# Moving the start addresses of the buffers that TensorE reads

## The chip, the cores and the metric

The kernel runs on one core of one Trainium2 chip. The metric is the device time of one execution in microseconds, the median of several. A profiled execution gives, beside its own time, a trace: start and duration of the instructions of every engine. In the trace PE is TensorE at its matmuls, PEld is TensorE loading the stationary operand of a matmul (LDWEIGHTS, which overlaps the matmul ahead of it), DVE is VectorE, ACT is ScalarE, POOL is GpSimd, and SP issues the DMAs.

## The reference

A gated mix of an attention block and a GEGLU feed-forward block, both over the same input `x` of 2048 rows by 448 columns, in float32:

```python
g = _sigmoid((x * gate_w).sum(-1, keepdims=True))
a = _A_ref(x, A_wqkv, A_wo)        # 16 heads of 28: softmax(q k^T * 28**-0.5) v, then @ wo
b = _B_ref(x, B_w_gate, B_w_up, B_w_down)   # (gelu(x @ w_gate) * (x @ w_up)) @ w_down, 1792 wide
return g * a + (1 - g) * b
```

## The kernel before

**Precision.** Most products are made of two-part operands: each float32 value is split into a rounded part and the remainder, both of type float32r, and `PAIRS` names the 11 products of parts that make one full product over the 448 rows. So a block of 128 x 512 results is 11 matmuls one after the other into one PSUM tile. Only the product of exponentials and V is plain float32; its matmuls stand in the trace as two records each.

**Stages.** First, `X` (both parts of x transposed, resident for the whole kernel) is loaded and Q and K are computed (`pqk`, 28 blocks) and written to DRAM in two parts; then V and the gate's sums (`pv`). Second comes attention: per head, `Q` and `K` (114 rows: four copies of the 28 values and two rows for a bound) are loaded into one of two sets of buffers, head by head in turn. For every 128 keys and half of the 2048 queries there are two matmuls `sc` (K block stationary, Q moving) into a PSUM tile of 1024 columns, of which there are three; ScalarE makes exponentials `pt` of it (12 buffers). After every eighth such tile come 32 records of `po` (V stationary, `pt` moving) for the 512 keys of the section before. `fill` strews the up-projection `pu` (weights `half` stationary, `X` moving) between the scores, two matmuls at a time, so that a section of eight score tiles holds 16 `sc` and 11 `pu` matmuls. Third comes the feed-forward part: `pg` (gate projection, again `half` stationary and `X` moving), its gelu multiplied by the stored `u`, the split product `hl2`, and `pd`: `hl2` stationary, the split down weights `w` moving, six matmuls for two weight tiles. In between, `project` multiplies the attention output `ohl` (stationary) with `WO` (moving), also into a `pd` tile.

**Weights in turn.** `load_half` (up and gate weights) and `load_f` (down weights) each go round three buffers, which are called `half0` to `half2` and `w0` to `w2`.

**The order.** The matmuls keep the order in which they are written (`keep_in_program_order`); the other engines' work is placed by the framework's dependencies and the pools' buffers.

**Where the buffers lie.** Each tile is a stretch of bytes in every SBUF partition. The allocator stacks the tiles of a pool, so a tile's first byte follows from the sizes of the tiles ahead of it. The widths in the code before carry `LINE = 16` extra floats (64 bytes) for several tiles, by which the start addresses are spread. Start addresses modulo 512 bytes, of the tiles which TensorE reads, worked out from the program's allocation:

| tile | role in its matmul | before | after |
|---|---|---|---|
| X | moving in pqk, pu, pg; stationary in pv | 352 | 352 |
| WQK | stationary in pqk | 352 | 352 |
| WV | moving in pv, rows of 1800 bytes | 352 | 352 |
| Q (two buffers) | moving in sc | 32, 32 | 352, 352 |
| K (two buffers) | stationary in sc | 32, 96 | 352, 352 |
| half (three buffers) | stationary in pu, pg | 352, 416, 480 | 352, 352, 352 |
| V | stationary in po, 128 bytes further per head | 32 | 352 |
| pt | moving in po | 352 | 352 |
| hl2 (four buffers) | stationary in pd | 32 | 352 |
| w first part (three buffers) | moving in pd | 288, 352, 416 | 352, 352, 352 |
| w second part | moving in pd | 32, 96, 160 | 352, 352, 96 |
| ohl | stationary in pd of `project` | 288 | 352 |
| WO, its eight blocks | moving in pd of `project` | 288 and 32 in turn | 352 |

Within X, Q, K, half and hl2 every matmul reads from an offset that is a multiple of 512 bytes, so the residue of the tile is that of each of its matmuls' operands. "Residue" below means this start address modulo 512.

Of the kernel before, what the change touches and what calls it, by code (L numbers as in the profile page):

```python
# [7 lines left out]
F32 = mybir.dt.float32  # L8
F32R = mybir.dt.float32r
I32 = mybir.dt.int32  # L10
AF = mybir.ActivationFunctionType
OP = mybir.AluOpType
# [4 lines left out]
S, D, H, DH, F = 2048, 448, 16, 28, 1792  # L17
P = 128
TB = 512
# [9 lines left out]
NB = 3  # L29
ORDER = (2, 3, 1, 4, 0, 5, 6)  # L30
NR = 4 * DH + 2
LINE = 16
VW = 450
SCALE = DH ** -0.5
BOUND = 20.0
# [8 lines left out]
def gated_mix(ctx: ExitStack, tc: tile.TileContext, xT, wqk, wvg, wg, wu, wd, wo, sel, ident, out):  # L44
    nc = tc.nc

    def mm(o, lhsT, rhs, start, stop):
        tc.keep_in_program_order(nc.tensor.matmul(o, lhsT, rhs, start=start, stop=stop))  # L48
# [13 lines left out]
    fw = ctx.enter_context(tc.tile_pool(name="fw", bufs=2))  # L62
# [1 line left out]
    vp = attn.enter_context(tc.tile_pool(name="vp", bufs=1))  # L64
    V = vp.tile([P, NKT, H, 32], F32, name="V")
    kq = attn.enter_context(tc.tile_pool(name="kq", bufs=1))
    heads = [tuple(kq.tile([NR, S + n * LINE], F32R, name=f"{x}{i}")[:, 0:S] for x, n in (("Q", i), ("K", 4 * i)))
             for i in range(2)]
    for _, K in heads:
        nc.gpsimd.memset(K[96:].bitcast(F32), 1.0)  # L70
    nc.gpsimd.memset(V[:, :, :, DH:], 1.0)
# [124 lines left out]
    with tc.If(bounded < 1):  # L196
        with ExitStack() as ph:
            gp = ph.enter_context(tc.tile_pool(name="gp", bufs=2))
# [4 lines left out]
            for h in range(H):  # L203
                Q = gp.tile([4 * DH, S], F32R, name="gQ")
                K = gp.tile([4 * DH, S], F32R, name="gK")
# [3 lines left out]
                for i in range(NT):  # L209
                    p = gps.tile([P, S], F32, name="gsc")  # L210
# [14 lines left out]
    gp = ctx.enter_context(tc.tile_pool(name="gp", bufs=1, side="right"))  # L225

    halves = {}

    def load_half(src, f, key, hi):
        raw = fw.tile([P, 4, P], F32, name="hraw")  # L230
        w = fw.tile([P, 8 * P + LINE], F32R, name=f"half{len(halves) % 3}", bufs=1)
        w = w[:, 0:8 * P].rearrange("p (w n) -> p w n", w=8)
        nc.sync.dma_start(out=raw, in_=src[f])
        hi(w[:, 0:4], raw)
        nc.vector.tensor_tensor(w[:, 4:8], raw, w[:, 0:4].bitcast(F32), OP.subtract)
        halves[key, f] = w
# [5 lines left out]
    with ExitStack() as ph:  # L242
# [52 lines left out]
        def up():  # L295

            todo = [(wu, f, "u") for f in range(NF)] + [(wg, f, "g") for f in range(NB)]
            load_half(*todo[0], nc.vector.tensor_copy)
            for n, (_, f, key) in enumerate(todo):
                for tb in range(NTB):  # L300
                    if tb == 1 and n + 1 < len(todo):
                        load_half(*todo[n + 1], nc.vector.tensor_copy)
                    s = slice(tb * TB, (tb + 1) * TB)
                    p = psu.tile([P, TB], F32, name="pu")
                    for i, (x, w) in enumerate(PAIRS):
                        mm(p, halves[key, f][:, w], X[:, x, s], i == 0, i == len(PAIRS) - 1)
                        if i < len(PAIRS) - 1:
                            yield False
                    u = op.tile([P, TB], F32, name="u")
                    nc.vector.tensor_copy(u, p)  # L310
                    nc.sync.dma_start(out=ud[n, :, s], in_=u)
                    yield True
# [47 lines left out]
    with ExitStack() as ph:  # L360
# [3 lines left out]
        tp = ph.enter_context(tc.tile_pool(name="tp", bufs=3, reuse_waits="tile"))  # L364
        wpo = ph.enter_context(tc.tile_pool(name="wpo", bufs=1, reuse_waits="tile"))
        psg = ph.enter_context(tc.tile_pool(name="psg", bufs=3, space=PSUM, reuse_waits="tile"))
        psd = ph.enter_context(tc.tile_pool(name="psd", bufs=5, space=PSUM, reuse_waits="tile"))
        WD = {}

        def load_f(f):  # L370
            if f >= NB:
                load_half(wg, f, "g", by_act)
            draw = gp.tile([P, D], F32, name="draw")
            w = gp.tile([P, 2 * D + LINE], F32R, name=f"w{len(WD) % 3}", bufs=1)
            w = w[:, 0:2 * D].rearrange("p (a n) -> p a n", a=2)
            nc.sync.dma_start(out=draw, in_=wd[f * P:(f + 1) * P])
            nc.scalar.activation(w[:, 0], draw, AF.Copy)
            nc.vector.tensor_tensor(w[:, 1], draw, w[:, 0].bitcast(F32), OP.subtract)
            WD[f] = w

        def hidden(f, tb, hl):
            s = slice(tb * TB, (tb + 1) * TB)
# [15 lines left out]
        def down(c, tb, hls):  # L398
            for i in range(4):
                t = tb * 4 + i  # L400
                s = slice(i * P, (i + 1) * P)
                p = psd.tile([P, D], F32, name="pd")
                n = 3 * len(hls)
                k = 0
                for f, hl in hls:
                    for a, b in ((0, 0), (1, 0), (0, 1)):
                        mm(p, hl[:, a, s], WD[f][:, b], k == 0, k == n - 1)
                        k += 1
                g1 = gate[:, 2, t:t + 1]
                if c == 0:  # L410
                    nc.vector.tensor_scalar(acc[:, t], p, g1, None, OP.mult)
                elif c < NF // FC - 1:
                    nc.vector.scalar_tensor_tensor(acc[:, t], p, g1, acc[:, t], OP.mult, OP.add)  # L413
                else:
                    y = tp.tile([P, D], F32, name="y")
                    nc.vector.scalar_tensor_tensor(y, p, g1, acc[:, t], OP.mult, OP.add)  # L416
                    nc.sync.dma_start(out=out[0, t * P:(t + 1) * P], in_=y)


        WO = wpo.tile([P, 8, D], F32R, name="WO")  # L420
        OHL = {}

        def load_wo():
            raw = wpo.tile([P, 4, TB], F32, name="oraw")[:, :, 0:D]
            nc.sync.dma_start(out=raw, in_=wo)
            nc.scalar.activation(WO[:, 0:4], raw, AF.Copy)
            nc.vector.tensor_tensor(WO[:, 4:8], raw, WO[:, 0:4].bitcast(F32), OP.subtract)

# [15 lines left out]
        def project(tb):  # L444
            O = OHL[tb]
            for i in range(4):
                t = tb * 4 + i
                p = psd.tile([P, D], F32, name="pd")
                for k, (x, w) in enumerate(PAIRS):
                    mm(p, O[:, x, i * P:(i + 1) * P], WO[:, w], k == 0, k == len(PAIRS) - 1)  # L450
                nc.vector.scalar_tensor_tensor(acc[:, t], p, gate[:, 1, t:t + 1], acc[:, t], OP.mult, OP.add)

        order = [f for c in ORDER for f in range(c * FC, (c + 1) * FC)]
        load_f(order[0])
        pend = None
        for n in range(NF // FC):
            for tb in range(NTB):
                hls = []
                for k in range(n * FC, (n + 1) * FC):
                    if tb == 0 and k + 1 < NF:  # L460
                        load_f(order[k + 1])
                    hl = hp.tile([P, 2, TB], F32R, name="hl2", bufs=4)
                    hidden(order[k], tb, hl)
                    hls.append((order[k], hl))
                if pend:
                    down(*pend)
                pend = n, tb, hls
                if n == 1 and tb == 0:
                    load_wo()
                if n in (2, 3) and tb % 2 == 0:  # L470
                    load_o((n - 2) * 2 + tb // 2)
                if n in (2, 3) and tb % 2 == 1:
                    project((n - 2) * 2 + tb // 2)
        down(*pend)


# [33 lines left out]
```

## Time and profile before

| | |
|---|---|
| time, median of 3 runs | 1064.3 us (1063.98 to 1065.54) |
| the profiled execution's own time | 1065.08 us |
| its span, first to last instruction | 1063.3 us |
| granted TensorE clock, mean | 0.999 |
| PE busy | 1049.6 us, 99%, 5664 records |
| ACT busy | 616.4 us, 58% |
| DVE busy | 319.2 us, 30% |
| DMA, mean | 109 GB/s |

The span is what the trace covers; the execution's own time is 1.78 us longer. A group's row reads: line, engine, operation, output<-inputs, shapes, count, then busy time in us and the mean duration of one in ns, then idle time of the engine ahead of them. All matmuls are issued by the helper `mm` in line 48, so they are told apart by their tiles. A matmul's recorded duration reaches into the next one's: successive matmuls overlap in the record, so the busy time of a group without gaps, divided by its count, is the step from one matmul to the next, and the mean duration is longer than that by a constant part.

### The profile page before, as it was taken

To read this page: it belongs to the slowest core of one execution; us is meant where nothing else is said; L and a number is where in the kernel's file an instruction comes from. 1 tells how busy PE (TensorE), PEld (TensorE's weight loads), DVE (VectorE), ACT (ScalarE), POOL (GpSimd) and SP (SyncE) were. 2 spreads that over 40 slices of the span, in tenths; PEclk is the share of its full clock that TensorE was granted. 3 is DMA by queue.
4 is the path that set the end of the run, shared out by engine and by line. 5 is a ranking of instruction groups with operands and counts; after the bars stand their busy time and mean duration, and the time that the engine had idled before them with its cause. 6 is when DMAs were issued, how large, how long until landed. Compare 5 with 4: busy or idle time off the path is not lost.

```text
span 1063.3 us, 14546 instructions
## 1 busy us (share of the span) xinstructions
PE 1049.6 (99%) x5664; PEld 732.8 (69%) x5664; DVE 319.2 (30%) x519; ACT 616.4 (58%) x732; POOL 41.0 (4%) x32
## 2 busy tenths in 40 slices
PE   7999999999999999999999999999999999999998
PEld 6789755656556556556566565565588888899887
DVE  5561111111011111110110110111156756577555
ACT  5322478778777777777787787787634322233321
POOL 5300000000000000000000000000001002100000
PEclk9999999999999999999999999999999999999999
DMA  8875222432332332232232232331164322342233
GB/s 278 283 273 131 66 67 73 125 99 73 103 103 73 98 109 73 94 112 73 94 112 74 94 105 80 94 94 50 51 196 140 108 90 90 97 149 67 61 87 119
DMA packets 58907, 115.85 MB, mean 109 GB/s; under 512 B 12784, under 2 KB 18160, under 8 KB 55216
## 3 DMA queue, kind: packets, MB, share of 16 engines
q1 hardware_dynamic: 58832, 114.85, 35.0%
q8 instruction: 47, 0.77, 0.3%
q14 instruction: 28, 0.23, 0.1%
HBM read 74.44 MB, written 40.37 MB: 108 GB/s over the span
## 4 chain that ended last, share of the span: by engine, by line
PE 88%; DVE 0%; issue 0%; DVEq 0%
PE sc L48 24%; PE po L48 21%; PE pu L48 16%; PE pd L48 16%; PE pg L48 11%; DVE u L310 0%; DVE y L416 0%; DVE gate L180 0%; DVE gate L179 0%; DVE gate L181 0%; DVEq L310 0%
## 5 line engine op out<-in xcount | busy, mean ns | idle before, releaser
L264 ACT ACTIVATE pt<-sc 128x1024 f32<-128x1024 f32 x512 | 482.6, 1026 | 163.9 <-PE sc L48 163.2
L48 PE MATMUL sc<-Q,K 114*128 114x512 f32 x1024 | 317.7, 402 | 1.2 <-issue 1.2
L48 PEld LDWEIGHTS sc<-Q,K 114*128 114x128 f32 x1024 | 188.6, 189 | 94.0 <-issue 54.4
L48 PE MATMUL pu<-X,half 128*128 128x512 f32 x748 | 237.3, 396 | 0.6 <-PEq L196 0.3
L48 PE MATMUL po<-pt,V 128*32 128x512 f32 x2048 | 233.0, 595 | 0.0
L310 DVE COPY u<-pu 128x512 f32<-128x512 f32 x68 | 47.0, 692 | 492.3 <-PE pu L48 485.3
L48 PEld LDWEIGHTS pu<-X,half 128*128 128x128 f32 x748 | 140.9, 189 | 35.5 <-issue 1.6
L48 PEld LDWEIGHTS po<-pt,V 128*32 128x32 f32 x2048 | 60.0, 109 | 138.2 <-issue 132.4
L48 PE MATMUL pd<-w,hl 128*128 128x448 f32 x672 | 140.0, 365 | 0.0
L48 PEld LDWEIGHTS pd<-w,hl 128*128 128x128 f32 x672 | 126.2, 188 | 11.1
L48 PE MATMUL pg<-X,half 128*128 128x512 f32 x484 | 115.5, 393 | 0.0
L48 PEld LDWEIGHTS pg<-X,half 128*128 128x128 f32 x484 | 91.0, 188 | 19.6
L48 PE MATMUL pqk<-X,WQK 128*128 128x512 f32 x308 | 73.5, 400 | 7.6 <-ACT X L107 6.0
L48 PEld LDWEIGHTS pqk<-X,WQK 128*128 128x128 f32 x308 | 59.1, 193 | 21.7 <-ACT X L107 6.2
L393 ACT ACTIVATE g<-pg 128x512 f32<-128x512 f32 x44 | 26.1, 594 | 71.1 <-PE pg L48 71.0
L394 DVE TENSOR_TENSOR g<-g,u 128x512 f32<-128x512 f32 x56 | 46.1, 831 | 52.2 <-ACT g L393 52.1
L395 ACT ACTIVATE hl<-g 128x512 fp32r<-128x512 f32 x56 | 35.2, 630 | 42.8 <-DVE g L394 37.1
L413 DVE SCALAR_TENSOR_TENSOR acc<-pd,gate,acc 128x448 f32<-128x448 f32 x80 | 52.8, 679 | 6.0 <-PE pd L48 6.0
L441 POOL TENSOR_TENSOR ohl<-oraw,ohl 128x1536 fp32r<-128x1536 f32 x4 | 14.0, 3506 | 752.9 <-ACT ohl L437 752.9
L396 DVE TENSOR_TENSOR hl<-g,hl 128x512 fp32r<-128x512 f32 x56 | 38.2, 687 | 10.7 <-ACT hl L395 8.7
L48 PE MATMUL pv<-WV,X 128*128 128x450 f32 x176 | 36.5, 367 | 0.0
L48 PE MATMUL pd<-WO,ohl 128*128 128x448 f32 x176 | 36.3, 365 | 0.0
(60 smaller groups left out, 324.0 us busy)
## 6 DMA issues: line engine op xcount, KB each, us to landing
ud<-u SPq DMA_DIRECT2D x68, 256.0 KB
qkd<-hl SPq DMA_DIRECT2D x28, 512.0 KB
Q<-qkd SPq DMA_DIRECT2D x64, 224.0 KB
K<-qkd SPq DMA_DIRECT2D x64, 224.0 KB
u<-ud SPq DMA_DIRECT2D x56, 256.0 KB
raw<-in_xT SPq DMA_DIRECT2D x16, 256.0 KB
rb<-rdend SPq DMA_DIRECT2D x64, 64.0 KB
hraw<-in_wu SPq DMA_DIRECT2D x14, 256.0 KB
```

Source lines behind the costliest of these rows:

```text
L48: tc.keep_in_program_order(nc.tensor.matmul(o, lhsT, rhs, start=start, stop=stop))
L264: nc.scalar.activation(pt, sc, AF.Exp, scale=SCALE)
L310: nc.vector.tensor_copy(u, p)
L393: nc.scalar.activation(g, pg, AF.Gelu_apprx_tanh)
L394: nc.vector.tensor_tensor(g, g, u, OP.mult)
L395: nc.scalar.activation(hl[:, 0], g, AF.Copy)
L396: nc.vector.tensor_tensor(hl[:, 1], g, hl[:, 0].bitcast(F32), OP.subtract)
L413: nc.vector.scalar_tensor_tensor(acc[:, t], p, g1, acc[:, t], OP.mult, OP.add)
L441: nc.gpsimd.tensor_tensor(O[:, 4:7], o[:, 0:3], O[:, 0:3].bitcast(F32), OP.subtract)
```

## The change

The start addresses of the last column of the table above. Nothing else: the same instructions follow each other on every engine with the same kinds of waits. The two instructions that write the split `WO` now write four rows of 448 with a pitch of 512 instead of one row of 1792. The extra floats go from `Q`, `K` and `half`; the three `half` buffers become one tile name with three buffers; the down weights' tile is widened so that its second part begins 2048 bytes after the first (in the third buffer the first part begins 256 bytes into the tile); `WO` gets rows of 512 floats; and `y`, which TensorE doesn't read, is widened to 512 floats so that what is stacked behind it keeps its residue.

```diff
@@ -64,8 +63,7 @@
-    heads = [tuple(kq.tile([NR, S + n * LINE], F32R, name=f"{x}{i}")[:, 0:S] for x, n in (("Q", i), ("K", 4 * i)))
-             for i in range(2)]
+    heads = [tuple(kq.tile([NR, S], F32R, name=f"{x}{i}") for x in "QK") for i in range(2)]
@@ -228,8 +226,7 @@
         raw = fw.tile([P, 4, P], F32, name="hraw")
-        w = fw.tile([P, 8 * P + LINE], F32R, name=f"half{len(halves) % 3}", bufs=1)
-        w = w[:, 0:8 * P].rearrange("p (w n) -> p w n", w=8)
+        w = fw.tile([P, 8, P], F32R, name="half", bufs=3)
@@ -370,13 +367,16 @@
+            n = len(WD) % 3
+            size, hi, lo = ((TB + D, 0, TB), (TB + D, 0, TB), (TB + D + 32, 64, 64 + D))[n]
+            w = gp.tile([P, size], F32R, name=f"w{n}", bufs=1)
             draw = gp.tile([P, D], F32, name="draw")
-            w = gp.tile([P, 2 * D + LINE], F32R, name=f"w{len(WD) % 3}", bufs=1)
-            w = w[:, 0:2 * D].rearrange("p (a n) -> p a n", a=2)
             nc.sync.dma_start(out=draw, in_=wd[f * P:(f + 1) * P])
-            nc.scalar.activation(w[:, 0], draw, AF.Copy)
-            nc.vector.tensor_tensor(w[:, 1], draw, w[:, 0].bitcast(F32), OP.subtract)
-            WD[f] = w
+            hi, lo = w[:, hi:hi + D], w[:, lo:lo + D]
+            nc.scalar.activation(hi, draw, AF.Copy)
+            nc.vector.tensor_tensor(lo, draw, hi.bitcast(F32), OP.subtract)
+            WD[f] = hi, lo
@@ -404,7 +404,7 @@
-                        mm(p, hl[:, a, s], WD[f][:, b], k == 0, k == n - 1)
+                        mm(p, hl[:, a, s], WD[f][b], k == 0, k == n - 1)
@@ -412,12 +412,12 @@
-                    y = tp.tile([P, D], F32, name="y")
+                    y = tp.tile([P, TB], F32, name="y")[:, 0:D]
-        WO = wpo.tile([P, 8, D], F32R, name="WO")
+        WO = wpo.tile([P, 8, TB], F32R, name="WO")[:, :, 0:D]
```

More of the change, by code (lines that the diff above doesn't have):

```diff
@@ L31 @@
 NR = 4 * DH + 2
-LINE = 16
 VW = 450
```

## The prediction

> **What bounds the kernel now.** I read the page's table of engines first, then the chain of work that ended last.
>
> ```profile
> PE 1049.6 (99%) x5664; PEld 732.8 (69%) x5664; DVE 319.2 (30%) x519; ACT 616.4 (58%) x732; POOL 41.0 (4%) x32
> PEclk9999999999999999999999999999999999999999
> PE 88%; DVE 0%; issue 0%; DVEq 0%
> PE sc L48 24%; PE po L48 21%; PE pu L48 16%; PE pd L48 16%; PE pg L48 11%; DVE u L310 0%; DVE y L416 0%; DVE gate L180 0%; DVE gate L179 0%; DVE gate L181 0%; DVEq L310 0%
> ```
>
> TensorE works without a gap at full granted clock, and the chain is its matmuls alone. So neither a wait nor a transfer sets the end: the time is the number of matmuls times the step from one to the next. The instructions and their order stay, so only the step can change. The question is whether it depends on start addresses, and the trace before already holds both cases.
>
> **Does the step depend on addresses?** The stage that computes Q and K reads X and WQK, both at residue 352. From the groups of PE in the window 55 to 100 us:
>
> ```profile
> L48 PE MATMUL pqk<-X,WQK 128*128 128x512 f32 x116 | 26.5, 389 | 0.0
> ```
>
> The records overlap, and only the last one's 389 ns reach beyond its own step, by 0.16 us; so the step is (26.5 - 0.16)/116 = 227.1 ns. The gate projection has the same shapes and the same X, but its weights go round three buffers at 352, 416 and 480. From the chain of waits in order of time, 800 to 860 us:
>
> ```profile
> 815.40 4.86 PE pd L48 x24
> 820.26 5.10 PE pg L48 x22
> 825.36 4.85 PE pd L48 x24
> 830.21 5.12 PE pg L48 x22
> ...
> 850.14 2.51 PE pg L48 x11
> 852.65 4.85 PE pd L48 x24
> ```
>
> By the turn of the buffers, the pieces of 22 pair `half1` with `half2`; the piece of 11 is `half0` alone. The steps: 5.12/22 = 232.7 ns, and 2.51/11 = 228.2 ns. So the same matmul is 4.5 to 5.6 ns (2%) shorter where both operands start at one residue. The 228.2 holds the entry from `pd`, which reads other residues; between it and the 227.1 of the long stream I take **227.7 ns** for an agreeing step in mixed work.
>
> A rule of the Trainium skill speaks against this. "SBUF — State Buffer", section "Who interferes with whom", says that PE and ACT never wait on anyone, and "TensorE: Matmul & The Clock Gate", step-by-step in Part 2, that loading the next weights takes no read bandwidth from the running matmul. By them the change would be worth nothing; the two pg steps above do not agree, as their order, shape and clock are alike.
>
> **Attention: scores and up-projection.** Here Q reads at 32, K at 32 (even heads) or 96 (odd ones), X at 352 and `half` at its three residues; two `sc` and two `pu` alternate, so operands of different residues meet at every second step. All groups of PE between 160 and 735 us:
>
> ```profile
> L48 PE MATMUL sc<-Q,K 114*128 114x512 f32 x915 | 284.5, 402 | 0.0
> L48 PE MATMUL po<-pt,V 128*32 128x512 f32 x1824 | 207.5, 595 | 0.0
> L48 PE MATMUL pu<-X,half 128*128 128x512 f32 x631 | 202.9, 395 | 0.0
> ```
>
> and one section in the timeline of PE:
>
> ```profile
> 395.55 3.64 PE L48 MATMUL po<-pt,V 128*32 128x512 f32 x32
> 399.12 0.73 PE L48 MATMUL sc<-Q,K 114*128 114x512 f32 x2
> 399.69 0.63 PE L48 MATMUL pu<-X,half 128*128 128x512 f32 x2
> ...
> 404.38 0.40 PE L48 MATMUL pu<-X,half 128*128 128x512 f32 x1
> 404.61 1.10 PE L48 MATMUL sc<-Q,K 114*128 114x512 f32 x4
> 405.64 0.64 PE L48 MATMUL po<-pt,V 128*32 128x512 f32 x4
> ```
>
> The `po` blocks by the chain of waits in order of time, in heads 0, 1, 3 and 4:
>
> ```profile
> 143.71 3.57 PE po L48 x32
> ...
> 194.11 3.57 PE po L48 x32
> ...
> 264.73 3.57 PE po L48 x32
> 325.09 3.57 PE po L48 x32
> ```
>
> From 399.69 to 404.38 are 20 steps: 234.5 ns each. The first two and last four `sc` of the section take 0.57 + 1.03 = 1.60 us instead of 6 x 0.2345 = 1.41, so the passage into `po` and out of it costs 0.19 more. Over the 575 us of the window: 1824/32 = 57 sections; 575 - 57 x (3.57 + 0.19) = 360.7 us for 915 + 631 = 1546 steps: **233.3 ns**. If agreement does here what it does in pqk and pg, each saves 5.6 ns. Of 1024 + 748 steps some 128 are passages, which I leave as they are: 1644 x 5.6 = **9.2 us**. Bounds: nothing, or 6.2 ns down to pqk's 227.1: 10.2 us.
>
> `po` stays. V lies 128 bytes further for each head, so heads 0, 1, 3 and 4 read it at 32, 160, 416 and 32; each piece is 3.57 us all the same. Moving V to 352 changes nothing: 0.
>
> **Gate projection.** Of its 44 tiles 28 use `half1` or `half2`: 308 steps x (232.7 - 227.7) = 1.5 us; the 176 of `half0` win 0.5 ns each on their entries, 0.1. Together **1.6 us**; bounds 0.8 (only to 228.2 plus half of that lost again) and 2.0.
>
> **Down and output products.** 672 + 176 matmuls of 448 columns. The `pd` pieces above are 4.85/24 = 202.1 ns a step, and none has moving and stationary operand agreeing throughout, so the trace has no price. Bounds: nothing, and pg's 5.0 ns for all 848, 4.2 us. `hl2` at 32 agreed with itself and with the second part of `w` in one buffer of three, so less is left than in pg; and afterwards the second part in the third buffer still begins at 96, which mixes residues in four of seven rounds. I take 2 ns for three quarters of them: **1.3 us**.
>
> **What stays.** pqk and pv read as before. The two writes of WO get a pitch; they are one instruction each on ACT and DVE, with TensorE busy beside them: 0. Were that cover gone they would cost what they cost now, since the element count is the same. DMAs, DVE and ACT work keep count and size.
>
> **Sum.** 9.2 + 1.6 + 1.3 = 12.1 us. Span 1063.3 - 12.1 = 1051.2; the execution around it is 1.78 us longer, 1053.0. The profiled execution (1065.08) stood 0.8 above the median of 1064.3, so I predict a median of **1052.3**. By the bounds this case alone runs from 1050 to 1056.
>
> **Rivals.**
>
> *ScalarE takes over in attention* (10%). A score tile needs the exponential three tiles before it. Where `sc` comes closest to this, before each `po` (rows of the timelines of ACT and PEld, then the page's group):
>
> ```profile
> 399.94 6.63 ACT L264 ACTIVATE pt<-sc 128x1024 f32<-128x1024 f32 x7 [2.55 <-PE sc L48]
> ...
> 403.69 1.97 ACT L264 ACTIVATE pt<-sc 128x1024 f32<-128x1024 f32 x2
> ...
> 404.85 0.19 PEld L48 LDWEIGHTS sc<-Q,K 114*128 114x128 f32 x1
> ...
> 405.56 1.94 ACT L264 ACTIVATE pt<-sc 128x1024 f32<-128x1024 f32 x2
> ...
> L264 ACT ACTIVATE pt<-sc 128x1024 f32<-128x1024 f32 x512 | 482.6, 1026 | 163.9 <-PE sc L48 163.2
> ```
>
> The exponential that began at 403.69 (1026 ns, the first of that pair) ends at 404.72, and the weight load for which it frees the tile starts at 404.85: 0.13 us of slack. Seven steps lie between that exponential's start and the load, so agreement takes 7 x 5.6 = 0.04 of it. Against a stall: the pair of 1.94 us shows that exponentials can follow each other every 1.94 - 1.03 = 0.91 us, and four agreeing steps take 0.911. For it: that is no reserve at all, and seven in a row came every (6.63 - 1.03)/6 = 0.933. If ScalarE can't hold 0.91, the fifth exponential's end stays put and a section gains only from the slack, some 0.07 of 0.13 us: 64 x 0.07 = 4.5 instead of 9.2, and 1064.3 - 7.4 = 1056.9.
>
> *Only unbroken streams gain* (7%). Alternating X and Q, and 114 with 128 rows, could break what agreement gives even at one residue. Then pg and pd alone pay: 1064.3 - 2.9 = 1061.4. Against it: pqk changes its X block and its weight tile all the time and keeps 227.1.
>
> *Addresses do nothing* (7%): pg's difference would then come from its neighbours or the DMA traffic at that time, and the steps stay: 1064.3. Against it: three buffers taken in turn give two steps that keep to the buffer. By the Trainium skill's rule above this would be the case to expect.
>
> *Agreement costs in attention* (8%, the other side). From the groups of PE in four-section windows, `half1` (268.8 to 308.9 us) and then `half0` (349.3 to 389.5 us):
>
> ```profile
> L48 PE MATMUL pu<-X,half 128*128 128x512 f32 x44 | 14.1, 394 | 0.0
> L48 PE MATMUL pu<-X,half 128*128 128x512 f32 x44 | 14.2, 397 | 0.0
> ```
>
> Where X and `half` agree, `pu` is 2 to 3 ns longer, the reverse of pg. I read it as the price of coming from Q at 32. If it is the pairing itself that is bad behind a score, all 1644 steps lose 2.5 ns, 4.1 us; pg still wins 1.6 and pd nothing: 1066.8. It decides if `pu` keeps 397 with Q at 352.
>
> **How the numbers follow.** The forecast holds 68%. About 0.2%, 2.1 us, is what this kernel's measurement tells from no change (the three runs span 1.6 us). Forecast, ScalarE and unbroken streams are faster by more: 68 + 10 + 7 = 85%; same 7%; slower 8%. The range reaches from below full agreement with most of pd's bound, 1049.5, over the ScalarE and the streams cases to 1062.0; what lies outside is the two cases without a gain and a little of each tail.
>
> **What would show it.** In the changed kernel's profile: `sc` and `pu` near 390 ns where they stand between each other, a section of 10.09 us (395.55 to 405.64) down to about 9.95, pieces of 22 pg all near 5.02, `po` still at 3.57, the mean of `pd` a little under 365. Wrong would be: rows of PEld waiting for ACT `pt` in every section (ScalarE), pg at 5.02 with `sc` and `pu` unchanged (streams only), or 5.12 still there.

## The result, and the profile after

| | before | changed |
|---|---|---|
| median, timed side by side (12 runs each) | 1065.05 us | 1063.61 us |
| span of the profiled execution | 1063.3 us | 1062.1 us |

The ratio is 0.9984, with a 95% interval of 0.9975 to 0.9993: a gain of 1.4 us where 12 were forecast. From the page of the changed kernel, the table of engines and the chain:

```profile
PE 1048.9 (99%) x5664; PEld 732.3 (69%) x5664; DVE 321.0 (30%) x519; ACT 617.1 (58%) x732; POOL 41.3 (4%) x32
PE 88%; DVE 0%; issue 0%; DVEq 0%
```

TensorE still sets the end alone, with 0.7 us less busy time. Where the forecast saw most of the gain, in attention, nothing moved. The groups of PE between 160 and 735 us in the changed kernel (line, engine, operation, output<-inputs, shapes, count, then busy us and mean ns of one):

```profile
L47 PE MATMUL sc<-Q,K 114*128 114x512 f32 x915 | 284.3, 402 | 0.0
L47 PE MATMUL po<-pt,V 128*32 128x512 f32 x1824 | 207.5, 595 | 0.0
L47 PE MATMUL pu<-X,half 128*128 128x512 f32 x631 | 203.2, 396 | 0.0
```

The counts are the same as before, the scores are at 402 ns as before, and `pu` at 396 instead of 395. One section in the timeline of PE:

```profile
395.53 3.64 PE L47 MATMUL po<-pt,V 128*32 128x512 f32 x32
399.10 0.73 PE L47 MATMUL sc<-Q,K 114*128 114x512 f32 x2
399.67 0.63 PE L47 MATMUL pu<-X,half 128*128 128x512 f32 x2
...
404.34 0.40 PE L47 MATMUL pu<-X,half 128*128 128x512 f32 x1
404.57 1.08 PE L47 MATMUL sc<-Q,K 114*128 114x512 f32 x4
405.59 1.92 PE L47 MATMUL po<-pt,V 128*32 128x512 f32 x16
```

From 399.67 to 404.34 are again 20 steps, 233.5 ns each where 234.5 stood, and the section lasts 10.06 us instead of 10.09. All four operands now begin at 352, and over the whole window the step is that of before, 233.3 ns by the forecast's own reckoning.

The gate projection did what was forecast. The chain of waits in order of time, 800 to 860 us:

```profile
819.83 5.02 PE pg L47 x22
824.85 4.86 PE pd L47 x24
829.71 5.02 PE pg L47 x22
...
849.47 2.52 PE pg L47 x11
```

Every piece of 22 is now 5.02 us, where 5.10 and 5.12 stood: 228.2 ns a step with any of the three buffers. The down products stay at 4.86/24 = 202.5 ns. The pages' groups give the sums, first of the kernel before, then of the changed one:

```profile
L48 PE MATMUL pd<-w,hl 128*128 128x448 f32 x672 | 140.0, 365 | 0.0
L48 PE MATMUL pg<-X,half 128*128 128x512 f32 x484 | 115.5, 393 | 0.0
```

```profile
L47 PE MATMUL pd<-w,hl 128*128 128x448 f32 x672 | 140.4, 365 | 0.0
L47 PE MATMUL pg<-X,half 128*128 128x512 f32 x484 | 114.1, 390 | 0.0
```

So pg won 1.4 us, and attention gave nothing. The 0.4 us by which pd's sum is higher is no loss that the change explains: with the same down addresses it stands at 140.1 us in runs 2, 5, 6 and 7 below. The question for the experiments is why agreeing addresses shorten the step in pqk and pg, and not in attention or in the down products.

### The profile page after: what moved, and what is told of

It reads as the page before. It is cut to its first block, busy times and chain, and to the rows that moved or that the text cites. A ratio compares the mean times of both kernels' runs of the same rounds, so it can differ in the third digit from the quotient of the medians.

```text
span 1062.1 us, 14546 instructions
## 1 busy us (share of the span) xinstructions
PE 1048.9 (99%) x5664; PEld 732.3 (69%) x5664; DVE 321.0 (30%) x519; ACT 617.1 (58%) x732; POOL 41.3 (4%) x32
## 4 chain that ended last, share of the span: by engine, by line
PE 88%; DVE 0%; issue 0%; DVEq 0%
PE sc L47 24%; PE po L47 22%; PE pu L47 16%; PE pd L47 16%; PE pg L47 10%; DVE u L307 0%; DVE y L416 0%; DVE gate L178 0%; DVE gate L177 0%; DVE gate L179 0%; DVEq L307 0%
## 5 line engine op out<-in xcount | busy, mean ns | idle before, releaser
L47 PE MATMUL po<-pt,V 128*32 128x512 f32 x2048 | 233.0, 595 | 0.0
L47 PE MATMUL pd<-w,hl 128*128 128x448 f32 x672 | 140.4, 365 | 0.0
L47 PEld LDWEIGHTS pg<-X,half 128*128 128x128 f32 x484 | 90.9, 188 | 18.5
L47 PE MATMUL pqk<-X,WQK 128*128 128x512 f32 x308 | 74.2, 401 | 7.0 <-ACT X L105 5.5
L47 PE MATMUL pd<-WO,ohl 128*128 128x448 f32 x176 | 36.3, 365 | 0.0
```

## The experiments

Two things set attention apart from pg: its score matmuls use 114 rows of the array and its up-projection 128, and operands, PSUM tiles and kinds of accumulation alternate. The down products differ from pg by 448 moving columns and by stationary blocks that are written shortly before.

**1. Padding Q and K to 128 rows.** The added rows of Q are zero.

```diff
-NR = 4 * DH + 2
+NR = P
...
-    for _, K in heads:
+    for Q, K in heads:
         nc.gpsimd.memset(K[96:].bitcast(F32), 1.0)
+        nc.gpsimd.memset(Q[96:].bitcast(F32), 0.0)
...
-            nc.sync.dma_start(out=Q[4 * DH:].bitcast(F32), in_=shd[h])
+            nc.sync.dma_start(out=Q[4 * DH:4 * DH + 2].bitcast(F32), in_=shd[h])
```

> The changed kernel with Q and K padded from 114 to 128 rows (the added rows of Q are zero), so that every float32r matmul of attention uses the whole height of the array; addresses as in the changed kernel. Theory A (the step of 227 ns needs one and the same row count from matmul to matmul; going between 114 and 128 rows breaks it): sc and pu in attention fall from about 233.4 to 227 to 228 ns, a section from 10.07 to about 9.93 us, the time by 8 to 10 us to about 1054. Theory B (it is the alternation of operands, PSUM tiles or single-shot and accumulating matmuls that breaks it): sc and pu stay at 233 and the time at 1063.

Measured: 1059.06 us, ratio to the kernel before 0.9944 (0.9928 to 0.9959). The page's groups:

```profile
L47 PE MATMUL sc<-Q,K 128*128 128x512 f32 x1024 | 313.1, 397 | 1.4 <-issue 1.3
L47 PE MATMUL pu<-X,half 128*128 128x512 f32 x748 | 233.5, 391 | 0.4 <-DVE u L308 0.3
```

Over the whole kernel `sc` fell from 402 to 397 ns and `pu` from 396 to 391: theory A, against B. The padded matmuls do more work on the array, and each is 5 ns sooner done. The time fell less than the steps promise; the longest waits of PE in this run say where:

```profile
PE pqk L47 <- ACT X L106: 5.6, 2, 5.4
PE pqk L47 <- DVE mx L123: 3.4, 2, 3.1
```

The second was 1.5 us in the changed kernel. The longest of these waits ended at 24.77 us, and ahead of it one VectorE instruction on X took 5.01 us, while POOL worked on X and WV; in the changed kernel it took 1.69. From 20 to 30 us the granted clock was 0.83 in this run and 1.00 in the changed kernel, and `pqk`'s busy time rose from 74.2 to 75.5 us. Runs 5 to 7 follow that up.

**2. 114 rows in the scores, the up-projection and pg.** This kernel leaves out the last 14 rows of each block of `pu` and `pg`, so it is of use for its times alone.

```diff
-mm(p, halves[key, f][:, w], X[:, x, s], ...)
+mm(p, halves[key, f][0:NR, w], X[0:NR, x, s], ...)
...
-mm(pg, halves["g", f][:, w], X[:, x, s], ...)
+mm(pg, halves["g", f][0:NR, w], X[0:NR, x, s], ...)
```

> The changed kernel with pu and pg cut to 114 of their 128 rows (the products leave out the last 14 rows of each block), so that attention holds 114-row matmuls alone, and the gate projection is an unbroken stream of them. Theory A (changing the row count is what costs): pu and sc at 227 to 228 in attention, pg at 227; time about 1054. Theory A2 (114 rows are slow by themselves): pg rises from 228 to about 233 and attention stays at 233; time about 1065. Theory B (alternation): pg at 227 to 228, attention unchanged at 233; time about 1063.

Measured, one execution: 1056.57 us, span 1054.8. The page's groups:

```profile
L47 PE MATMUL sc<-Q,K 114*128 114x512 f32 x1024 | 313.6, 398 | 1.3 <-issue 1.2
L47 PE MATMUL pu<-X,half 114*128 114x512 f32 x748 | 234.8, 393 | 0.8 <-PEq L194 0.5 <-DVE u L307 0.3
L47 PE MATMUL pg<-X,half 114*128 114x512 f32 x484 | 113.9, 390 | 0.0
```

`sc` is untouched here, 114 rows as in the changed kernel, and yet 4 ns shorter, because its neighbours now have 114 rows as well. So 114 rows are not slow in themselves, and neither is alternation: it is the passage from one row count to another. (`pu`'s 393 holds a stretch at a lower clock: from 120 to 130 us the granted clock was 0.83. Between 160 and 735 us, at 1.00, `pu` is at 390 and `sc` at 397. pg shows 390 with either row count.)

**3. The down products with 512 moving columns.** Both parts of `w` get 512 columns, 64 of them zeros, at residue 352 in all three buffers; one buffer of `o` makes room.

```diff
-            w = gp.tile([P, size], F32R, name=f"w{n}", bufs=1)
+            w = gp.tile([P, 2 * TB + (32 if n == 2 else 0)], F32R, name=f"w{n}", bufs=1)
+            nc.gpsimd.memset(w[:, D:TB].bitcast(F32), 0.0)
+            nc.gpsimd.memset(w[:, TB + D:2 * TB].bitcast(F32), 0.0)
...
-            WD[f] = hi, lo
+            WD[f] = w[:, 0:TB], w[:, TB:2 * TB]
...
-                p = psd.tile([P, D], F32, name="pd")
+                p = psd.tile([P, TB], F32, name="pd")
```

> The changed kernel with the moving operand of the down products widened from 448 to 512 columns (64 columns of zeros, not used), both parts of all three weight buffers at residue 352. Theory C (the short step needs a moving operand whose length is a multiple of 512 bytes, so that each matmul ends where the next begins modulo 512; 448 columns are 1792 bytes): the down steps come out at 227 ns like pg, and pg has no entry of longer steps after them; the output product, left at 448 columns, stays at 202.7. Theory D (the down products lack something else, such as stationary blocks that are written shortly before): their step is 232 to 234 ns. In both the time rises, by 672 x 24 to 31 ns: 16 to 21 us.

Measured, one execution: 1080.1 us. The chain of waits in order of time, 800 to 850 us:

```profile
802.05 4.99 PE pg L47 x22
807.03 5.44 PE pd L47 x24
812.48 4.99 PE pg L47 x22
```

5.44/24 = 226.7 ns for the down steps, theory C; and pg at 4.99/22 = 226.8 lost the rest of its entry (it was 228.2 behind 448-column steps). Freshly written stationary blocks do no harm here. The residue of the third buffer's second part moved too, from 96; but the rounds over the other two buffers agreed throughout in the changed kernel already, and all its `pd` pieces of 24 took 4.86 or 4.87 us. With 448 columns no start address that was tried changes the step: 140.0 us with six residues, 140.1 to 140.4 with one for most of it, and `WO` is at 36.3 us with 288 and 32 in turn as with 352. Whether it is the length modulo 512 bytes that counts, or something else about 448, was not tried with a third length at one residue.

**4. The `half` buffers alone.** The kernel before, with a pad that keeps every other tile at its old address.

```diff
+    vp.tile([P, 48], F32, name="pad")
...
-        w = fw.tile([P, 8 * P + LINE], F32R, name=f"half{len(halves) % 3}", bufs=1)
-        w = w[:, 0:8 * P].rearrange("p (w n) -> p w n", w=8)
+        w = fw.tile([P, 8, P], F32R, name="half", bufs=3)
...
+        ap.tile([P, 48], F32, name="pad2")
```

> The kernel before with the three half buffers alone moved to residue 352 (a pad keeps every other tile at its old address). If the whole gain of the change is the gate projection's: pg falls from 230.9 to 228.0 ns, 1.4 us, attention stays within 0.3 us, and the time is the changed kernel's, ratio to the kernel before 0.998 to 0.999. If Q, K, V or the down weights have a part in it, less than the 1.1 us by which the changed kernel's span is shorter.

Measured: 1064.41 us, ratio 0.9987 (0.9978 to 0.9996), span 1063.0. The page's groups:

```profile
L48 PE MATMUL pu<-X,half 128*128 128x512 f32 x748 | 239.4, 399 | 0.4 <-DVE u L310 0.3
L48 PE MATMUL pg<-X,half 128*128 128x512 f32 x484 | 113.8, 390 | 0.0
```

pg has its whole gain, 1.7 us; but `pu`, with X and `half` agreeing and Q and K at other residues, rose by 2.1 us, where at most 0.3 was expected. Not all of this is the step. The groups of PE from 160 to 735 us have this row:

```profile
L48 PE MATMUL pu<-X,half 128*128 128x512 f32 x629 | 203.2, 397 | 0.0
```

So `pu` is at 397 there, against 395 before and 396 in the changed kernel. But from 100 to 160 us its mean is 423 ns, against 401 before: from 120 to 130 us the granted clock was 0.83, and 1.00 in the kernel before and the changed one. About half of the 2.1 us is thus the clock of this execution (18.5 us for 58 `pu` before 160 us, against 18.3 for 61), and what the addresses do to `pu` here is 1 to 2 ns. In the trace gain and rise nearly cancel, and the span is 0.3 us shorter than before; the timed runs say 1.4 us. The two intervals, of this run and of the changed kernel, overlap, so the share of the other tiles is not settled by the timed runs.

**5 to 7. Getting the padding out of the first stage's way.** Run 5 is run 1 with the two fills of Q written behind the stage of Q and K. The framework placed them early all the same, on either side of POOL's first cast of X.

> As the run with 128 rows, but the two fills of Q's added rows with zeros stand on POOL behind the Q and K stage instead of ahead of the first X blocks. Theory: the 4.9 us by which that run's first stage was longer (pqk's long steps 15.0 instead of 10.1 us) come from these two fills of 1.8 us each ahead of POOL's first work on X. Then pqk's long steps return to about 10 us, sc and pu stay at 227.9 ns, and the time is 9 to 10 us under the changed kernel's: about 1054, ratio to the kernel before 0.990. Rival: the first stage only scatters from run to run (its long steps were 8.8 to 11.8 us in the other runs), then the gain over the first run with 128 rows is 3 to 6 us by chance and the place of the fills has nothing to do with it; POOL's rows and the start of the X work tell.

Measured: 1060.47 us, ratio 0.9957 (0.9944 to 0.9971). The profiled execution was the fastest, 1056.42; the others, 1060.2 to 1061.0, have no trace. So the expected 1054 was missed and the place of the fills still undecided. Run 6 made the zeros as X times zero on POOL.

```diff
+    for Q, _ in heads:
+        nc.gpsimd.tensor_scalar(Q[96:], X[96:, 0].bitcast(F32), 0.0, None, OP.mult)
```

> The changed kernel with 128-row Q and K once more; the zeros in Q's added rows are now made as X times zero, so that they must wait for X, and every instruction of PE, ACT, DVE and SP stands where it stands in the changed kernel (in the two runs before, the fills ahead of or between POOL's first X work also moved ACT and SP work of the first stage). Theory: the 9.4 us that sc and pu win per execution then show in the time: span about 1052.5, time about 1054 to 1055, ratio to the kernel before 0.989 to 0.991. Rival: something else of the padding, such as 32 rows in place of 18 in the fills of K, costs the first stage 4 to 6 us in most executions; then the median stays near 1060 and pqk's long steps are over 14 us.

Measured: 1060.21 us, ratio 0.9957 (0.9944 to 0.9971). Timelines of POOL and of PE around 50 us:

```profile
43.01 10.82 POOL L190 TENSOR_SCALAR Q<-X 32x2048 fp32r<-32x2048 f32 x2
53.91 2.99 POOL L112 TENSOR_TENSOR X<-raw,X 128x512 fp32r<-128x512 f32 x2
```

```profile
49.83 2.81 PE L47 MATMUL pqk<-X,WQK 128*128 128x512 f32 x11 [0.25 <-DVE mx L122]
57.03 29.30 PE L47 MATMUL pqk<-X,WQK 128*128 128x512 f32 x121 [4.39 <-DVE mx L122]
```

The two operations took 5.4 us each; TensorE went on at 57.03, after 4.39 us of idling. It had done 187 matmuls, 17 of the 28 blocks of Q and K, and stood among those of the third part of X, which it was reading already. So it didn't wait for POOL's remaining work on the fourth part, as the expectation for run 7 has it, but for VectorE, as the row says. The timeline of DVE:

```profile
49.69 4.43 DVE L233 CAST half<-hraw 128x512 fp32r<-128x512 f32 x1
...
56.30 0.68 DVE L122 TENSOR_REDUCE mx<-pqk 128x1 f32<-128x512 f32 x1
```

The cast of `half`, 0.42 us in the changed kernel, lasted until 54.12, just past the end of POOL's two operations at 53.83. Behind it came the `mx` that frees a PSUM tile of `pqk`; it ended at 56.98. From 50 to 60 us the granted clock was 0.85. Wait and clock together are the 4 to 5 us by which the time was too long: `pqk` waited 11.6 us in all and was busy for 74.7, against 7.6 and 74.2 in run 7. In each of the three places tried, the fills on POOL left the median 3.5 to 4.9 us above run 7's. Run 7 makes the zeros on DVE from V, which can't begin before Q and K are computed; they ran at 92.3 us.

```diff
+    for Q, _ in heads:
+        nc.vector.tensor_scalar(Q[96:], V[96:, 0:4].rearrange("p a h d -> p (a h d)"), 0.0, None, OP.mult)
```

> The changed kernel with 128-row Q and K; the zeros in Q's added rows are made on DVE as V times zero from the first four blocks of V, so they must come after the Q and K stage (in the run before, POOL made them from 43 to 54 us, ahead of its last work on X, and TensorE waited 4.4 us for that). PE, ACT and SP keep the changed kernel's order, POOL loses the fills. Theory: sc and pu at 227.9 ns, pqk's long steps back at 9 to 11 us, span 1052 to 1053, time 1054 to 1055, ratio to the kernel before 0.989 to 0.991. Rival: the time stays at 1060, then the gain of 9.4 us in attention is lost somewhere behind the first stage, and its windows show where.

Measured: **1055.55 us, ratio 0.9904 (0.9887 to 0.9921)**: faster than both kernels, by 9.9 us against the one before. Span 1053.9. The section in the timeline of PE, and the waits of PEld for ScalarE:

```profile
396.27 0.73 PE L47 MATMUL sc<-Q,K 128*128 128x512 f32 x2
396.84 0.63 PE L47 MATMUL pu<-X,half 128*128 128x512 f32 x2
...
401.39 0.39 PE L47 MATMUL pu<-X,half 128*128 128x512 f32 x1
401.62 1.07 PE L47 MATMUL sc<-Q,K 128*128 128x512 f32 x4
402.62 3.64 PE L47 MATMUL po<-pt,V 128*32 128x512 f32 x32
```

```profile
PEld sc L47 <- ACT pt L263: 0.8, 2, 0.5
```

From 396.84 to 401.39 are 20 steps of 227.5 ns, where 227.7 was forecast for the change itself, and ScalarE keeps up: two short waits in the whole kernel, as before.

**8. Rows without addresses.** The kernel before with 128 rows. A first run had its fills where run 5 has them.

> The kernel before, with its old addresses, and Q and K padded to 128 rows in the same way. If equal row counts are enough: sc and pu at 227 to 229 ns, the time near 1054. If addresses must agree as well (the reading of pg, where half1 and half2 took 233 and half0 228): sc and pu stay at 232 to 234, the time at 1063 to 1066.

It took 1066.35 us, ratio 1.0012 (1.0003 to 1.0021). A second had them where run 6 has them:

> The kernel before, old addresses, 128 rows made in the same way, first stage left in its order. Rows alone, without agreeing addresses: sc 232.2 and pu 231.0 ns as in the first run of this kind, that is 2.6 us less than the kernel before, a time of 1062 to 1063, ratio 0.997 to 0.999; were rows enough by themselves it would be 1055.

Measured: 1066.92 us, ratio 1.0028 (1.0016 to 1.0040). Groups of the second run, and its wait in the first stage:

```profile
L48 PE MATMUL sc<-Q,K 128*128 128x512 f32 x1024 | 316.7, 401 | 1.6 <-issue 1.6
L48 PE MATMUL pu<-X,half 128*128 128x512 f32 x748 | 235.8, 394 | 0.4 <-DVE u L312 0.3
```

```profile
PE pqk L48 <- DVE mx L124: 4.5, 1, 4.5
```

The row counts alone win 1 to 2 ns a step, 2.5 us in the groups' sums. The expected 1062 to 1063 was missed, because the fills on POOL cost more than that: the cast of `half` took 4.47 us here, too, and the clock was 0.83 from 50 to 60 us. Equal rows are not enough.

**9. Agreement within each matmul only.** Run 5 with Q and K at residue 32, X and `half` at 352.

```diff
+    kq.tile([P, 48], F32, name="pad")
     heads = [tuple(kq.tile([NR, S], F32R, name=f"{x}{i}") for x in "QK") for i in range(2)]
```

> As the run with the late fills, but Q and K (all four buffers) at residue 32, X and half at 352: moving and stationary operand of each matmul agree, but from a score to an up-projection matmul the residue jumps, at every second step. If agreement within a matmul is enough: sc and pu at 227.9. If all neighbouring matmuls must share one residue, since the next weights are read while the last moving operand is: 230 to 235 ns, and the time 4 to 10 us above that run's.

Measured, one execution: 1067.71 us, span 1065.9. The page's groups:

```profile
L47 PE MATMUL sc<-Q,K 128*128 128x512 f32 x1024 | 317.4, 402 | 1.1 <-issue 1.1
L47 PE MATMUL pu<-X,half 128*128 128x512 f32 x748 | 235.3, 393 | 0.7 <-PEq L197 0.4 <-DVE u L310 0.3
```

402 and 393 instead of 397 and 391: it is not enough that a matmul's own operands agree; neighbours must share the residue. (By the order of the pools the pad also shifts what is stacked behind K, WQK and `pt` among it; `po`'s sum stays at 233.0 us.) The rest of its time is the first stage again: 4.7 us of waiting for VectorE's `mx`, behind an instruction of 6.10 us on X, and a clock of 0.83 from 20 to 30 us.

**The steps side by side.** Between 160 and 735 us the granted clock was 1.00 in all these runs. Reckoned as in the forecast, 3.76 us for each 32 records of `po` taken off, the window gives:

| run | row counts | residues | `sc` + `pu` | `po` records | step, ns |
|---|---|---|---|---|---|
| before | 114, 128 | mixed | 915 + 631 | 1824 | 233.3 |
| changed | 114, 128 | all 352 | 915 + 631 | 1824 | 233.3 |
| 4 | 114, 128 | `half` and X alone | 914 + 629 | 1824 | 233.8 |
| 8, second | 128 | mixed | 916 + 631 | 1840 | 231.9 |
| 9 | 128 | 32 and 352 in turn | 914 + 629 | 1852 | 231.6 |
| 2 | 114 | all 352 | 926 + 636 | 1856 | 228.5 |
| 7 | 128 | all 352 | 926 + 636 | 1856 | 228.5 |

## Why the prediction was wrong

*What bounds the kernel, order, `po`: right.* TensorE alone sets the end in all runs, and `po` has 3.57 us in every section of run 7 as of the kernel before.

*The step of 227.7 ns for agreeing addresses: right in value, wrong in its conditions.* pg came out at 228.2 behind `pd`, and 226.8 behind matmuls of its own length (run 3). The forecast put the longer entry down to the residues that `pd` reads; by these two runs it is `pd`'s length.

*Gate projection, 1.6 us forecast: 1.4 measured.*

*Attention, 9.2 us forecast: nothing measured.* This is the step that failed: "If agreement does here what it does in pqk and pg, each saves 5.6 ns". Both pqk and pg are streams of matmuls of one height, 128 rows. In attention the height goes from 114 to 128 and back at every second step, and with that the step is 233.3 ns at the old addresses and at the new. Runs 1 and 2 show it from both sides; with equal heights nearly the whole term is there: in run 7 `sc` and `pu` take 8.4 us less than in the changed kernel, and the span is 8.2 us shorter. The rival "only unbroken streams gain" named the heights as a possible cause and had 7%; its reason against, that pqk changes its blocks all the time and stays short, spoke of addresses and blocks, not of heights.

*Down and output products, 1.3 us forecast: nothing measured (140.0 us before, 140.1 to 140.4 at the new addresses; `WO` 36.3 in both).* The sum charged a gain of 2 ns a step by the nearness to pg; with 448 columns there is none (run 3). Zero was one end of the bounds, and nothing but that nearness spoke for the other.

*Rivals.* Addresses are not without effect: pg won. ScalarE doesn't take over even at 227.5 ns. That agreement itself costs in attention, read from `half0`'s 397 ns: the 4.1 us didn't come, as `sc` and `pu` sum to 555.0 us in both kernels. In the windows that the prediction compares, `pu` is at 396 with either buffer in the changed kernel, where 394 and 397 stood. So at two heights agreement evens the step out and doesn't shorten it; with equal heights `pu` goes to 391, and agreement costs nothing. That the 397 was the price of coming from Q at 32 is likely, but not shown apart from the heights.

The Trainium skill's rule, in "SBUF — State Buffer", section "Who interferes with whom", that PE never waits on anyone, would have come nearest for the wrong reason: the time moved by 0.16%, but TensorE's step does depend on where its operands lie, by 233 against 228 ns in pg, and by 231.9 against 228.5 in attention at 128 rows (run 8 against run 7).

## What to carry to other kernels

Where TensorE is the bound and its matmuls follow each other without a gap, look at the step from one to the next, group by group: a group that runs 2% over the shortest step of the same shape is worth a look at start addresses modulo 512 bytes, at the row counts of neighbouring matmuls and at the moving length. In attention these had to agree together; addresses alone gave nothing there and row counts alone 1 to 2 ns a step, so a trace of a stream that has two of them does not price a stage that lacks the third. And a helper operation in a tight first stage can cost up to half of what it is meant to bring, by way of another engine that TensorE waits for: give it a dependency that keeps it out. Before a mean over a whole execution is read as a step, look at the granted clock of its stretches: in runs 2 and 4, 10 us at 0.83 moved `pu`'s mean by 1 to 2 ns.

## What the runs showed of the hardware

Matmuls of 128 x 512 float32r, each with its own weight load, follow each other every 226.7 to 228.5 ns with one residue, one row count and 512 columns, and every 231 to 235 otherwise; pg's pieces of 22, with one residue, average 228.2 ns a step behind matmuls of 448 columns and 226.8 behind 512. Why it is so, no run here shows: only that, with one residue, the row count of the neighbour matters and not the row count itself, and that 128 rows next to 128 are 5 ns sooner done than 114 next to 128 (397 against 402 ns). POOL took 5.4 us for a multiplication over 32 rows of 2048 float32, DVE 1.22 us for the same (run 7), and POOL's plain fill of the same rows 1.80 us. Instructions of DVE lasted longer while POOL worked: a cast of 128 x 512 took 4.43 us in run 6 and 0.42 in the changed kernel; by what the two hinder each other, these runs don't show. In runs 1, 6, 8 and 9 the granted clock was 0.78 to 0.85 in the 10 us in which a pause of TensorE of 3.1 to 4.9 us ended. In runs 2 and 4 it was 0.83 from 120 to 130 us, where TensorE idles in every run; there it stayed at 1.00 in the others.
